# The first layer norm of the last row group, done by features instead of by rows

## The chip, the cores and the metric

The kernel runs on one core of one Trainium2 chip. The metric is the device time of one execution in microseconds (us); lower is better. All arithmetic is float32, or float32 split into a high and a low half that TensorE takes in its one-pass format (called fp32r in the rows of the profile).

## The reference

A transformer block with a modulated layer norm, 2048 rows of 448 features, 16 heads of 28:

```python
mod = (silu(c) @ w_mod).reshape(1, 6, 1, 448)
sa, ca, ga, sb, cb, gb = (mod[:, i] for i in range(6))
h = layernorm(x) * (1 + ca) + sa          # first norm
x = x + ga * attention(h, wqkv, wo)
h = layernorm(x) * (1 + cb) + sb
x = x + gb * gmlp(h, w_in, w_sp, b_sp, w_out)
```

`layernorm` is over the 448 features of a row, `(x - mean) / sqrt(var + eps)`. The change touches the first norm alone, and of it the last quarter of the rows.

## The kernel before, in words

The kernel is one program with its order written out by hand: each engine runs its instructions in the order in which the code issues them, and tiles wait for one another by semaphores. All DMAs that matter here go out on SyncE's queue (SP), also in order; each of eight semaphores of that queue is used in turn, so an issue can also wait for the DMA eight places before it.

The rows are handled in four groups g of 512. For each group the first norm makes `hT[g]`, the normalised rows turned so that features lie on the partitions: four blocks c of 128 features (the fourth has 64, held twice), each as a high half (`hi`) and a low half (what `hi` leaves out). TensorE (PE) then uses `hT[g]` for V (`v_tile`, four per group, 11 matmuls each) and for Q and K (`qk_unit`, seven per group, 11 matmuls each, of which only two per group are done ahead of the attention for g of 1 to 3). The order on PE in the stretch of interest is: V tiles 8 and 9 (g = 2), 16 transposes of group 3, V tiles 10 and 11, four matmuls that sum the modulation (`mod_sum`), Q/K units 0 and 3 of group 2, the same two of group 3, V tiles 12 to 15, another four sums, and then the first row maxima of the attention (`m_mm`, tile `mt`) woven into the other Q/K units.

How the norm of a group g is made:

- `load_x` brings 512 rows, four per partition. VectorE (DVE) takes mean and variance of each row (`ln_stat`), GpSimd (POOL) makes `rs = (var + eps) ** -0.5` (`rstd_of`, two instructions).
- `ln_norm`: DVE makes `xn = (x - mean) * rs`, four instructions, each followed by a small copy on ScalarE (ACT).
- `ln_transpose`: PE turns `xn` with 16 transposes into four PSUM banks; for each block c, ACT makes the full value with the modulation as scale and bias (`hfull`, line 118) and the high half (line 125), and DVE the low half (line 82).

`ln_next(g)` is called once for each g of 1 to 3, for 2 and 3 after two of the V tiles of group g - 1. It transposes group g and, between the blocks, takes the statistics of group g + 1. For g = 3, where no group follows, it calls `mod_split(1, ...)` after block c = 2 instead: ACT makes two high halves `acc_h`, POOL two low halves `acc_l`, and the four matmuls of `mod_sum` (line 260) read them. Their results go to `bc_ga` (DVE, line 264) and through a row in memory to `col_sb` (DVE line 268, SP lines 269 and 272).

`mod_acc(pair, k)` are DVE steps that multiply weights by `silu(c)` and add up. `pads(0, ...)` are DVE and POOL memsets (lines 574 to 576) of the first head's K and Q tiles `kst`, `qst`; the DMAs of `load_head` (lines 585 and 587) that fill these tiles wait for them, and the first `mt` matmul waits for those DMAs.

Of the kernel before, what the change touches and what calls it, by code (L numbers as in the profile page):

```python
# [8 lines left out]
F32 = mybir.dt.float32  # L9
F32R = mybir.dt.float32r  # L10
AF = mybir.ActivationFunctionType
ALU = mybir.AluOpType
# [8 lines left out]
NG = 4  # L21
# [9 lines left out]


@with_exitstack
def tile_adaln_mha_gmlp(ctx, tc, x, wqkv, wo, w_in, w_spT, b_sp, w_out, cT, w_mod0, w_mod, out):
# [6 lines left out]
    scr = ctx.enter_context(tc.tile_pool(name="scr", bufs=1, space=DRAM))  # L41
# [15 lines left out]
    cols = {}  # L57
# [23 lines left out]
    def sub(eng, dst, a, hi):  # L81
        eng.tensor_tensor(out=dst, in0=a, in1=hi.bitcast(F32), op=ALU.subtract)  # L82
# [16 lines left out]
    def rstd_of(var, rs, n):  # L99

        pool.tensor_scalar(out=rs, in0=var, scalar1=EPS, scalar2=None, op0=ALU.add)
        pool.tensor_tensor(out=rs, in0=rs, in1=mhalf[:, :n], op=ALU.pow)

    def ln_transpose(xns, full_pool, dsts, scol, bcol, engs, los=(pool,) * 4, mid=None, after=None):

        tps = []
        for c in range(4):
            tp = bank("tp")
            tps.append(tp)
            for t in range(4):  # L110
                pe.transpose(tp[:, t * 128 : (t + 1) * 128], xns[t][:, c * 128 : (c + 1) * 128], ident)  # L111
        if mid:
            mid()
        for c in (0, 2, 1, 3):
            tp = tps[c]
            f = full_pool.tile([128, 512], F32, name="hfull")
            if engs[c] is act:
                act.activation(f, tp, AF.Identity, scale=scol[:, c : c + 1], bias=bcol[:, c : c + 1])
            else:
                engs[c].tensor_scalar(  # L120
                    out=f, in0=tp, scalar1=scol[:, c : c + 1], scalar2=bcol[:, c : c + 1], op0=ALU.mult, op1=ALU.add
                )
            hi = dsts[:, c if c < 3 else 6, :]
            if engs[c] is act:
                act.activation(hi, f, AF.Copy)
# [24 lines left out]
    e1 = early.enter_context(tc.tile_pool(name="e1", bufs=2))  # L150
# [28 lines left out]
    def load_x(g, eng):  # L179
        xg = e1.tile([128, 4, D], F32, name="xg")  # L180
        for t0, t1 in ((0, 1), (1, 2), (2, 4)) if g == 0 else ((0, 4),):
            (act if t1 - t0 == 1 else eng).dma_start(xg[:, t0:t1, :], x[g, :, t0:t1])
        for t in range(4):
            xts[4 * g + t] = xg[:, t, :]

# [59 lines left out]
    def mod_split(pair, eng, pool_l, tag_l, bufs_l):  # L245

        acc = accs.pop(pair)
        accs[pair] = []
        for part in range(2):
            h = stage.tile([128, 512], F32R, name="acc_h", tag="qf")[:, :D]  # L250
            l = pool_l.tile([128, D], F32R, name="acc_l", tag=tag_l, bufs=bufs_l)
            act.activation(h, acc[:, part, :], AF.Copy)
            sub(eng, l, acc[:, part, :], h)
            accs[pair].append((h, l))

    def mod_sum(pair, part):

        pc = bank("pc")
        for i, a in enumerate(accs[pair][part]):
            pe.matmul(pc[:, :D], ones_r, a, start=i == 0, stop=i == 1)  # L260
        return pc[:, :D]

    def mod_bc(nm, pair, part):
        dve.tensor_copy(bcs[nm], mod_sum(pair, part))

    def mod_col(nm, pair, part, plus1):
        row, dst = e2.tile([1, D], F32, name="row"), scr.tile([D], F32, name=f"{nm}_scr")
        dve.tensor_scalar(out=row, in0=mod_sum(pair, part)[0:1], scalar1=plus1, scalar2=None, op0=ALU.add)
        sp.dma_start(dst.rearrange("(o n) -> o n", o=1), row)
        for r, e, c in ((0, 128, slice(0, 3)), (0, 64, slice(3, 4)), (64, 128, slice(3, 4))):  # L270
            src = dst[0:384] if e - r == 128 else dst[384:D]
            sp.dma_start(cols[nm][r:e, c], src.rearrange("(c p) -> p c", p=e - r))

    mv1, xn1 = {}, {}

    def ln_stat(g, ts):
        if g not in mv1:
            mv1[g] = e1.tile([128, 4, 2], F32, name="mv"), e1.tile([128, 4], F32, name="rs")
        for t in ts:
            st = e1.tile([128, 6], F32, name="st", bufs=4)  # L280
            dve.bn_stats(out=st, in_=xts[4 * g + t])
            dve.bn_aggr(out=mv1[g][0][:, t, :], in_=st)
# [40 lines left out]
    def v_tile(kt):  # L323
        v_copy(*v_mm(kt))
# [212 lines left out]
    def ln_step(g, t):  # L537
        ln_stat(g, (t,))
        if t % 2:
            ln_rs(g, t - 1, t + 1)  # L540

    def ln_next(g):

        if g + 1 < NG:
            ln_transpose(
                xn1.pop(g), e1, hT[g], cols["ca"], cols["sa"], (act,) * 4, (dve,) * 4, None,
                lambda c: ln_step(g + 1, (0, 2, 1, 3).index(c)),
            )
# [13 lines left out]
    for g in range(1, NG):  # L562
        if g == 3:
            early.close()
            stk = att.enter_context(tc.tile_pool(name="stk", bufs=1))
            kq = [[stk.tile([128, S], F32R, name=f"{n}st{i}") for n in "kq"] for i in range(3)]
            kst, qst = [a[0] for a in kq], [a[1] for a in kq]
            npool = att.enter_context(tc.tile_pool(name="npool", bufs=2))
            late_s = ExitStack()
            late_l = late_s.enter_context(tc.tile_pool(name="late_l", bufs=2))  # L570

            def pads(i, eng):

                dve.memset(kst[i][64:128, :].bitcast(F32), 0.0)
                eng.memset(qst[i][64:128, :].bitcast(F32), 0.0)
                pool.memset(kst[i][64:86, :].bitcast(F32), 1.0)

            pads(0, dve)

            def load_head(h, c0=0, c1=S):  # L580
                k, q = kst[h % 3], qst[h % 3]
                if h > 2:
                    sp.dma_start(q[84:86, :].bitcast(F32), q[86:88, :].bitcast(F32))
                for r0, i in ((0, 0), (56, 1), (28, 0)):
                    sp.dma_start(k[r0 : r0 + 28, c0:c1].bitcast(F32), qk_scr[i][D + h * DH : D + (h + 1) * DH, c0:c1])
                for r0, i in ((0, 0), (28, 1), (56, 0)):
                    sp.dma_start(q[r0 : r0 + 28, c0:c1].bitcast(F32), qk_scr[i][h * DH : (h + 1) * DH, c0:c1])
# [12 lines left out]
        if g + 1 < NG:  # L600
            ln_next(g + 1)
        for k in range(2):
            v_tile(4 * g + 2 + k)
            if g == 2 and k == 1:
                mod_bc("ga", 1, 0)
                mod_col("sb", 1, 1, 0.0)
            if g == 1 or g == 2 and k == 1:
                mod_acc(g, k if g == 1 else 0)
        if g < 3:
            for k, m in enumerate((0, 3)):  # L610
                qk_unit((m,), g)
                mod_acc(g, 3 - g + k)
            if g == 2:
                mod_acc(g, 3)
# [887 lines left out]
```

## Time and profile before

| what | value |
|---|---|
| three runs | 1394.78, 1395.45 and 1396.0 us, median 1395.45 |
| the profiled execution | 1395.17 us, of which 1393.4 us are the span of its instructions |
| busy: PE / PE weight load / DVE / ACT / POOL | 100% / 71% / 74% / 56% / 21% of the span |
| TensorE clock granted | full, in all 40 slices |

A row of a timeline reads: start, length, engine, line, operation, output <- input, how many, and in brackets how long the engine had been idle before it and what ended that. A row of the chain of waits reads: start, length, what. A row of a group ends with its busy time, the mean ns of one, and the idle time before. A row of windows reads: the stretch, its length, the busy time (and number) on PE, PE weight load, DVE, ACT and POOL, the granted clock, the share of the DMA engines, and GB/s. "SPq" is SyncE's DMA queue: its rows show an issue, not the transfer.

### The profile page before, as it was taken

The page shows a single profiled execution, that of the slowest core. Times are in us where ns is not written, and L with a number is a line of the kernel's source. Part 1 is how long each engine was busy: PE and PEld are TensorE (multiplying, and loading weights), DVE is VectorE, ACT ScalarE, POOL GpSimd, SP SyncE. Part 2 cuts the span into 40 slices and gives each one's busy share as a digit, 9 for nine tenths or more (in the row PEclk, how much of TensorE's full clock was granted, in tenths as well). Part 3 has the DMA queues.
Part 4 walks back from the last instruction along what each step waited for, and adds up shares of the span by engine and source line. Part 5 has one row for each costly group of instructions (what it writes and reads, how often), then busy time and mean ns, then how long its engine had stood idle before and what let it go on. Part 6 is the DMA issues. An engine that isn't in the chain of part 4 may idle for free.

```text
span 1393.4 us, 20303 instructions
## 1 busy us (share of the span) xinstructions
PE 1388.3 (100%) x7170; PEld 988.5 (71%) x7170; DVE 1024.4 (74%) x1742; ACT 779.9 (56%) x1498; POOL 286.2 (21%) x306
## 2 busy tenths in 40 slices
PE   9999999999999999999999999999999999999998
PEld 8888655555555555555555555988998888888888
DVE  7798888888888888888888851850366655668574
ACT  6623677766666777777777779363234544434211
POOL 2144212221224243323200021000142430000000
PEclk9999999999999999999999999999999999999999
DMA  8464644655465556555323002434103333445453
GB/s 285 143 177 173 188 115 151 176 169 156 152 174 162 166 163 185 165 160 155 108 68 78 20 18 72 165 119 140 46 9 105 112 111 110 143 138 164 142 171 113
DMA packets 99489, 187.01 MB, mean 134 GB/s; under 512 B 17656, under 2 KB 29434, under 8 KB 96842
## 3 DMA queue, kind: packets, MB, share of 16 engines
q1 hardware_dynamic: 96670, 181.42, 43.0%
q10 hardware_dynamic: 2718, 4.30, 0.8%
q8 instruction: 56, 0.92, 0.3%
q14 instruction: 45, 0.37, 0.1%
HBM read 130.42 MB, written 50.46 MB: 130 GB/s over the span
## 4 chain that ended last, share of the span: by engine, by line
PE 98%; DMA 1%; DVE 0%; SPq 0%; POOL 0%; issue 0%; ACT 0%
PE st_ps L671 19%; PE o_ps L686 17%; PE mt L639 17%; PE acc L1246 7%; PE acc L1247 7%; PE acc L1248 7%; PE z_ps L1172 5%; PE z_ps L1058 5%; PE pq L335 5%; PE wo_ps L927 3%; PE pv L317 2%; PE y_ps L1353 2%; PE y_ps L1352 2%; PE y_ps L1354 2%; PE tp L111 1%; DMA xg<-in_x_dram 1%
## 5 line engine op out<-in xcount | busy, mean ns | idle before, releaser
L644 DVE TENSOR_REDUCE pm<-mt 128x1 f32<-128x512 f32 x1024 | 631.0, 682 | 85.9 <-PE mt L639 85.8
L675 ACT ACTIVATE P<-st_ps 128x512 f32<-128x512 f32 x1024 | 514.6, 632 | 201.7 <-PE st_ps L671 201.7
L671 PE MATMUL st_ps<-qst,kst 128*128 128x512 f32 x1024 | 404.4, 406 | 0.0
L639 PE MATMUL mt<-kst,qst 128*128 128x512 f32 x1024 | 402.4, 393 | 0.0
L671 PEld LDWEIGHTS st_ps<-qst,kst 128*128 128x128 f32 x1024 | 191.2, 187 | 141.1 <-issue 93.1
L686 PE MATMUL o_ps<-P,V 128*32 128x512 f32 x2048 | 247.1, 598 | 0.0
L639 PEld LDWEIGHTS mt<-kst,qst 128*128 128x128 f32 x1024 | 192.4, 188 | 31.8
L790 POOL TENSOR_TENSOR ws_raw<-ws_raw 128x512 f32<-128x512 f32 x80 | 103.1, 1289 | 293.5 <-DMA ws_raw<-in_w_spT_dram 293.4
L1134 ACT ACTIVATE wsp_h<-raw_sp 128x512 fp32r<-128x512 f32 x112 | 69.9, 631 | 153.5 <-PE acc L1248 104.0
L686 PEld LDWEIGHTS o_ps<-P,V 128*32 128x32 f32 x2048 | 54.6, 109 | 122.9 <-issue 114.6
L82 DVE TENSOR_TENSOR wsp_l<-raw_sp,wsp_h 128x512 fp32r<-128x512 f32 x112 | 80.6, 729 | 82.1 <-ACT wsp_h L1134 81.4
L1246 PE MATMUL acc<-wsp_h,heapA 128*128 128x512 f32 x224 | 87.3, 390 | 0.0
L1247 PE MATMUL acc<-wsp_l,heapA 128*128 128x512 f32 x224 | 87.2, 389 | 0.0
L1248 PE MATMUL acc<-wsp_h,heapA 128*128 128x512 f32 x224 | 87.2, 389 | 0.0
L1247 PE MATMUL acc<-wsp_l,heapB 128*128 128x512 f32 x174 | 67.7, 389 | 0.0
L1248 PE MATMUL acc<-wsp_h,heapB 128*128 128x512 f32 x174 | 67.7, 389 | 0.0
L1246 PE MATMUL acc<-wsp_h,heapB 128*128 128x512 f32 x174 | 67.7, 389 | 0.0
L335 PE MATMUL pq<-heapD,heapD 128*128 128x512 f32 x196 | 61.9, 390 | 0.0
L1176 DVE BATCH_NORM_STATS2 stz<-z 128x6 f32<-128x448 f32 x32 | 19.9, 625 | 50.4 <-ACT z L1175 29.8
L1246 PEld LDWEIGHTS acc<-wsp_h,heapA 128*128 128x128 f32 x224 | 42.1, 188 | 9.0 <-DVE cD L1252 0.3
L1248 PEld LDWEIGHTS acc<-wsp_h,heapA 128*128 128x128 f32 x224 | 42.0, 188 | 8.7
L1247 PEld LDWEIGHTS acc<-wsp_l,heapA 128*128 128x128 f32 x224 | 42.1, 188 | 8.5
(225 smaller groups left out, 1597.5 us busy)
## 6 DMA issues: line engine op xcount, KB each, us to landing
ws_raw<-in_w_spT_dram SPq DMA_DIRECT2D x160, 256.0 KB
ws_scr<-ws_raw SPq DMA_DIRECT2D x80, 256.0 KB
raw_sp<-ws_scr SPq DMA_DIRECT2D x80, 256.0 KB
kst<-qk_scr SPq DMA_DIRECT2D x45, 224.0 KB
qst<-qk_scr SPq DMA_DIRECT2D x45, 224.0 KB
raw_sp<-in_w_spT_dram SPq DMA_DIRECT2D x32, 256.0 KB
qk_scr<-qh SPq DMA_DIRECT2D x28, 256.0 KB
qk_scr<-ql SPq DMA_DIRECT2D x28, 256.0 KB
```

Source lines behind the costliest of these rows:

```text
L82: eng.tensor_tensor(out=dst, in0=a, in1=hi.bitcast(F32), op=ALU.subtract)
L335: pe.matmul(pq, wqk[:, b, m * 128 : (m + 1) * 128], hT[g][:, a, :], start=j == 0, stop=j == NST - 1)
L639: pe.matmul(mt, qst[h % 3][:, t * 128 : (t + 1) * 128], kst[h % 3][:, kb * 512 : (kb + 1) * 512], start=True, stop=True)
L644: dve.tensor_reduce(out=pms[h][:, t, kb : kb + 1], in_=mt, axis=AX.X, op=ALU.max)
L671: pe.matmul(st, kst[h % 3][:, kt * 128 : (kt + 1) * 128], qst[h % 3][:, qb * 512 : (qb + 1) * 512], start=True, stop=True)
L675: act.activation(p, st, AF.Exp, scale=SCALE)
L686: pe.matmul(otile[h][32 * qb : 32 * qb + 32, :], V[:, kt, h, :], ptiles.pop((u, qb)), start=kt == 0, stop=kt == NT - 1)
L790: pool.tensor_tensor(out=a, in0=a, in1=b, op=SUMS[i // 16][2])
L1134: act.activation(hi, raw, AF.Copy)
L1246: pe.matmul(acc[i], zh, hi, start=st == 0, stop=False)
L1247: pe.matmul(acc[i], zh, lo, start=False, stop=False)
L1248: pe.matmul(acc[i], zl, hi, start=False, stop=st == 7)
```

## The change

For group 3 the norm is done with the features on the partitions from the start. The host also lays out rows 1536 to 2047 turned (`xT`, four blocks of 128 features by 512 rows, the last block's 64 features twice), and once more by rows, with four neighbouring rows on each partition (`xs`). The statistics still come from the rows. POOL makes `rs` for all 512 rows at once; DVE makes `mr = -mean * rs`; both go to a scratch row in memory (each partition writes the 16 bytes of its four rows), and come back as two tiles `rows[0]` and `rows[1]`, the same 512 numbers on all 128 partitions. `ln_rank(c)` is two DVE instructions, `xc = xc * (1 + ca) * rs` and `xc = mr * (1 + ca) + xc`; `ln_fin(c)` is one on ACT (the high half, with `sa` as bias) and one on DVE (the low half). The 16 transposes, the eight ACT instructions on their results, the four of `ln_norm` and its four copies, and the four low halves of line 82 are gone for this group. `mod_split(1, ...)` now stands behind V tile 10.

```diff
     def load_x(g, eng):
...
-            (act if t1 - t0 == 1 else eng).dma_start(xg[:, t0:t1, :], x[g, :, t0:t1])
+            (act if t1 - t0 == 1 else eng).dma_start(xg[:, t0:t1, :], x[g, :, t0:t1] if g < 3 else xs)
...
+    def load_xT():
+        for c in (0, 2, 1, 3):
+            xcs[c] = e1.tile([128, 512], F32, name="xc", tag="xn", bufs=4)
+            sp.dma_start(xcs[c], xT[c])
+
+    def ln_rows(g):
+
+        mv, rs = mv1[g]
+        rstd_of(mv[:, :, 1], rs, 4)
+        mr = e1.tile([128, 4], F32, name="mr")
+        dve.scalar_tensor_tensor(out=mr, in0=mv[:, :, 0], scalar=-1.0, in1=rs, op0=ALU.mult, op1=ALU.mult)
+        dst = scr.tile([2, 512], F32, name="ln_scr")
+        for i, v in enumerate((rs, mr)):
+            sp.dma_start(dst[i].rearrange("(p t) -> p t", t=4), v)
+        for i in range(2):
+            rows.append(e1.tile([128, 512], F32, name="lnrow", tag="hfull"))
+            sp.dma_start(rows[i], dst[i].rearrange("(o n) -> o n", o=1).broadcast_to([128, 512]))
+
+    def ln_rank(c):
+        xc, a = xcs[c], cols["ca"][:, c : c + 1]
+        dve.scalar_tensor_tensor(out=xc, in0=xc, scalar=a, in1=rows[0], op0=ALU.mult, op1=ALU.mult)
+        dve.scalar_tensor_tensor(out=xc, in0=rows[1], scalar=a, in1=xc, op0=ALU.mult, op1=ALU.add)
+
+    def ln_fin(c):
+        xc, hi, b = xcs.pop(c), hT[3][:, c if c < 3 else 6, :], cols["sa"][:, c : c + 1]
+        act.activation(hi, xc, AF.Identity, bias=b)
+        r = slice(0 if c < 3 else 64, 128)
+        o = hT[3][:, 3 + c, :] if c < 3 else hi[r]
+        dve.scalar_tensor_tensor(out=o, in0=xc[r], scalar=b[r], in1=hi.bitcast(F32)[r], op0=ALU.add, op1=ALU.subtract)
+
     def ln_next(g):
 
-        if g + 1 < NG:
-            ln_transpose(
-                xn1.pop(g), e1, hT[g], cols["ca"], cols["sa"], (act,) * 4, (dve,) * 4, None,
-                lambda c: ln_step(g + 1, (0, 2, 1, 3).index(c)),
-            )
+        ln_transpose(
+            xn1.pop(g), e1, hT[g], cols["ca"], cols["sa"], (act,) * 4, (dve,) * 4, None,
+            lambda c: ln_step(g + 1, (0, 2, 1, 3).index(c)) if g == 1 else ln_stat(g + 1, ((0, 2, 1, 3).index(c),)),
+        )
+        if g == 1:
             ln_norm(g + 1, range(4))
         else:
-            ln_transpose(
-                xn1.pop(g), e1, hT[g], cols["ca"], cols["sa"], (act,) * 4, (dve,) * 4, None, lambda c: c == 2 and mod_split(1, pool, e1, "wm", 4)
-            )
+            load_xT()
+            ln_rows(g + 1)
...
-        if g + 1 < NG:
-            ln_next(g + 1)
+        if g == 1:
+            ln_next(2)
         for k in range(2):
+            if g == 2:
+                if k == 0:
+                    ln_rank(0)
+                    ln_rank(2)
+                    ln_fin(0)
+                else:
+                    ln_rank(1)
+                    ln_fin(2)
             v_tile(4 * g + 2 + k)
+            if g == 2 and k == 0:
+                mod_split(1, pool, e1, "wm", 4)
             if g == 2 and k == 1:
+                ln_rank(3)
+                ln_fin(1)
                 mod_bc("ga", 1, 0)
                 mod_col("sb", 1, 1, 0.0)
+                ln_fin(3)
             if g == 1 or g == 2 and k == 1:
                 mod_acc(g, k if g == 1 else 0)
```

More of the change, by code (lines that the diff above doesn't have):

```diff
@@ L33, in tile_adaln_mha_gmlp @@
 @with_exitstack
-def tile_adaln_mha_gmlp(ctx, tc, x, wqkv, wo, w_in, w_spT, b_sp, w_out, cT, w_mod0, w_mod, out):
+def tile_adaln_mha_gmlp(ctx, tc, x, xs, xT, wqkv, wo, w_in, w_spT, b_sp, w_out, cT, w_mod0, w_mod, out):
     nc = tc.nc
@@ L540, in ln_step @@
             ln_rs(g, t - 1, t + 1)
-    def ln_next(g):
-        if g + 1 < NG:
-            ln_transpose(
-                xn1.pop(g), e1, hT[g], cols["ca"], cols["sa"], (act,) * 4, (dve,) * 4, None,
-                lambda c: ln_step(g + 1, (0, 2, 1, 3).index(c)),
-            )
+    xcs, rows = {}, []
+    def load_xT():
[23 more added lines that the diff above has]
+        dve.scalar_tensor_tensor(out=o, in0=xc[r], scalar=b[r], in1=hi.bitcast(F32)[r], op0=ALU.add, op1=ALU.subtract)
+    def ln_next(g):
+        ln_transpose(
[3 more added lines that the diff above has]
+        if g == 1:
             ln_norm(g + 1, range(4))
         else:
-            ln_transpose(
-                xn1.pop(g), e1, hT[g], cols["ca"], cols["sa"], (act,) * 4, (dve,) * 4, None, lambda c: c == 2 and mod_split(1, pool, e1, "wm", 4)
-            )
+            load_xT()
+            ln_rows(g + 1)
     ln_next(1)
@@ L1462 @@
     cT[:64, 3] = cT[64:, 4] = _np.asarray(inputs["c"]).reshape(448)[384:]
+    xt = _np.asarray(inputs["A_x"])[0][1536:].T
     wm = _np.asarray(inputs["w_mod"]).reshape(448, 3, 2, 448)
@@ L1479 @@
         "x": _np.asarray(inputs["A_x"])[0].reshape(4, 4, 128, 448).transpose(0, 2, 1, 3),
+        "xs": _np.asarray(inputs["A_x"])[0][1536:].reshape(128, 4, 448),
+        "xT": _np.stack([xt[:128], xt[128:256], xt[256:384], _np.concatenate([xt[384:], xt[384:]])]),
         "wqkv": twice(inputs["A_wqkv"]),
```

## The prediction

> **What bounds the kernel now.** First the page's chain of work that ended last: it is TensorE nearly all the way, so a microsecond that TensorE gains or waits goes to the end one to one. Then that chain in order of time, around the change.
>
> ```profile
> PE 98%; DMA 1%; DVE 0%; SPq 0%; POOL 0%; issue 0%; ACT 0%
> ```
>
> ```profile
> 55.71 1.75 PE tp L111 x16
> 57.46 4.49 PE pv L317 x22
> 61.95 0.81 PE pc L260 x4
> 62.76 9.99 PE pq L335 x44
> ...
> 82.75 0.23 PE mt L639
> ```
>
> From 55.71 on PE goes from stretch to stretch with nothing between, up to the first row maximum at 82.75. Now the timelines of the engines beside it: DVE, then POOL.
>
> ```profile
> 49.96 0.18 DVE L282 BATCH_NORM_AGGREGATE mv<-st 128x2 f32<-128x6 f32 x1
> ...
> 52.44 0.68 DVE L235 TENSOR_SCALAR acc<-wm,silu 128x896 f32<-128x896 f32 x1
> ...
> 56.49 1.27 DVE L243 SCALAR_TENSOR_TENSOR acc<-wm,silu,acc 128x448 f32<-128x448 f32 x2
> ...
> 71.98 1.76 DVE L574 MEMSET kst<- 64x2048 f32 x1 [0.49 <-DVE acc L243]
> ```
>
> ```profile
> 24.75 0.59 POOL L101 TENSOR_SCALAR rs<-mv 128x4 f32<-128x4 f32 x1 [0.54 <-DVE mv L282]
> 25.42 1.33 POOL L102 TENSOR_TENSOR rs<-rs,mhalf 128x4 f32<-128x4 f32 x1
> ...
> 59.51 2.34 POOL L82 TENSOR_TENSOR acc_l<-acc,acc_h 128x448 fp32r<-128x448 f32 x2 [7.95 <-ACT acc_h L252]
> ```
>
> The last statistics are ready at 50.14, DVE's modulation work between ends at 57.76, and POOL's low halves for the four sums at 61.85: the third and fourth sums of the chain (62.35 to 62.76) have them with half a microsecond to spare. That is the one thing off PE that is close to it.
>
> **Part one, what goes.** The 16 transposes are 1.75 us of the chain. If nothing else is late, PE reaches the four sums at 55.71 + 4.49 = 60.20 instead of 61.95, and all behind it moves up by 1.75. The gain can be no more than that, 0.13% of the run.
>
> **Part two, what the rows now wait for.** The queue first, and the DMA windows.
>
> ```profile
> 43.16 2.01 SPq L171 DMA_DIRECT2D wm<-in_w_mod_dram  x4
> ...
> 64.48 0.29 SPq L269 DMA_DIRECT2D sb_scr<-row  x1
> 65.63 0.41 SPq L272 DMA_DIRECT2D col_sb<-sb_scr  x1
> ...
> 76.61 1.19 SPq L587 DMA_DIRECT2D qst<-qk_scr  x3
> ...
> 574.91 0.81 SPq L786 DMA_DIRECT2D ws_raw<-in_w_spT_dram  x2
> ...
> 708.83 0.35 SPq L706 DMA_DIRECT2D r_scr<-rt  x1
> 710.97 0.59 SPq L712 DMA_DIRECT2D rb<-r_scr  x1
> ```
>
> ```profile
> 578.77 1.29 POOL L790 TENSOR_TENSOR ws_raw<-ws_raw 128x512 f32<-128x512 f32 x1 [3.03 <-DMA ws_raw<-in_w_spT_dram]
> ```
>
> ```profile
> 43.00:50.00 7.00, 7.00 (x34) 6.04 (x33) 5.62 (x13) 5.28 (x9) 1.28 (x2) 1.00 0.99 320
> 50.00:54.00 4.00, 4.00 (x21) 3.59 (x20) 3.36 (x7) 2.21 (x7) 1.24 (x2) 1.00 0.01 4
> 76.00:81.00 5.00, 5.00 (x27) 4.60 (x26) 4.14 (x6) 1.59 (x4) 1.92 (x2) 1.00 0.80 194
> ```
>
> The `xT` blocks are four DMAs of 256 KB, 1.05 MB, issued behind the modulation weights (from 45.17). These keep the DMA engines full at 320 GB/s until 50; at that rate `xT` takes 3.3 us more, to 53.3, where now they idle (4 GB/s).
>
> POOL makes `rs` for four columns at once: 0.59 + 1.33, from 50.23 to about 52.2 (the two-column pair that it replaces let DVE's `xn` end just before 52.44, so DVE's next work starts as before). `rs` is issued at 52.25, `mr` about 0.4 later. A one-row write and the next issue that waits for it are 65.63 - 64.48 = 1.15 apart, a write of 128 rows of 64 bytes and the broadcast that waits for it 710.97 - 708.83 = 2.14. No row has 128 rows of 16 bytes; their count, not their bytes, is that of the second, so I take 2.14 (`rs` landed at 54.4) and keep 1.15 as the lower end (53.4). The upper end puts the rest of `xT` ahead of it in the same queue: 53.3 + 2.14 = 55.4. Since part of `xT` is surely ahead, I take 54.75, a third of the way from 54.4 to 55.4. Then the two tiles, 256 KB each: two loads of that size issued at 574.91 let the reader of the second start at 578.77, 3.86 later. So both tiles are there at about 54.75 + 3.8 = 58.55 (57.3 to 59.3 by the two ends).
>
> DVE is free for them at 57.76, so it is a near tie, and both lead to the same point. The prices come from the groups by form, in the stretch 40 to 90:
>
> ```profile
> L82 DVE TENSOR_TENSOR ql<-pq,qh 128x512 fp32r<-128x512 f32 x8 | 5.3, 687 | 2.3 <-ACT qh L348 2.3
> L237 DVE SCALAR_TENSOR_TENSOR acc<-wm,silu,acc 128x896 f32<-128x896 f32 x4 | 4.6, 1146 | 0.0
> L125 ACT ACTIVATE heapD<-hfull 128x512 fp32r<-128x512 f32 x8 | 5.1, 633 | 0.3
> L321 ACT ACTIVATE V<-pv 128x448 f32<-128x448 f32 x12 | 6.2, 544 | 6.4 <-PE pv L317 6.4
> L243 DVE SCALAR_TENSOR_TENSOR acc<-wm,silu,acc 128x448 f32<-128x448 f32 x4 | 2.6, 680 | 0.0
> L252 ACT ACTIVATE acc_h<-acc 128x448 fp32r<-128x448 f32 x4 | 2.1, 565 | 0.0
> ```
>
> The same DVE operation is 680 ns on 448 columns and 1146 on 896, so on 512 about 0.75; an instruction that doesn't need the one before starts some 0.08 ahead of its end (the pair at 56.49: 1.27 for two of 0.68). A `ln_rank`, two of which the second needs the first, is then about 1.45, the DVE half of `ln_fin` 0.67.
>
> **Part three, the wait that replaces the transposes.** The first `ln_rank` runs from 57.8 and needs `rows[1]` at 58.6: it ends at 59.35. ACT's next instruction is the high half of `ln_fin(0)`, which waits for that. Queued behind it on ACT are the copy of V tile 10, long finished on PE, and then `mod_split`, on which PE's four sums hang: 59.35 + 0.63 (high half) + 0.5 (copy) + 0.55 (first `acc_h`) = 61.05, POOL starts 0.1 later and takes 2.34 for both low halves: 63.45, against 61.85 before. PE, there at 60.2, waits for the last of them and starts the Q/K units at about 63.75, against 62.76: **1.0 later**, not 1.75 earlier. The cover that `mod_split` had, ACT with its inputs ready, is gone.
>
> **Part four, DVE up to the attention.** From 59.35 DVE has three more `ln_rank` (4.35), four low halves (2.7), `bc_ga` and the row (at most 0.68 each by the 448-column row, 1.2 with the overlap): 67.6. hT[3] is needed by PE at 63.75 + 5.0 (two units of the 9.99) = 68.75, so that is covered by 1.1. Behind it stand `mod_acc` and two low halves of Q/K: 0.68 + 0.69 + 1.15 + 0.69 + 1.15 + 1.27 = 5.6 less overlaps of 0.3, and the 0.49 that the memset waits: the first memset starts at about 73.4, against 71.98, 1.4 later. DVE, which idled between these steps before, no longer does. The `kst`/`qst` DMAs follow the memsets, so the last issue moves from 77.8 to 79.2. How near is the first `mt`, at 82.75? The six transfers of the first head are 6 x 168 KB = 1.03 MB; from 76 to 81 the engines moved 194 x 5 = 0.97 MB. So the loads are in only just before `mt` now. With the DMAs 1.4 later and PE 1.0 later, `mt` may wait another 0 to 0.4.
>
> **The sum.** +1.0 at the four sums, +0.3 at the first `mt`: **+1.3 us**. From there PE leads again and nothing takes it back. The profiled execution would be 1395.17 + 1.3 = 1396.5; the median of the runs stands 0.28 above it, so 1396.8.
>
> **A rule that speaks against the change.** While it waits at the sums, from 60.2 to 63.5, PE has three short matmuls. No row here shows PE so idle: in each of the windows above it is busy for the whole stretch at a granted clock of 1.00. The Trainium skill, page "TensorE: Matmul & The Clock Gate", section "Part 1: The HAM clock gate", says that the array's clock falls to half after an idle window of about 3.4 us and recovers after as long a busy one. By that page the sum would hold, if these few matmuls count as activity, and be a rival (the third below) if they don't.
>
> **The rivals.**
> 1. *The wait doesn't bite, about no change (1395.0 to 1395.9).* If the rows land by 57.3 and DVE and ACT hand over a little faster than I add up, the sums start 0.5 earlier, and the slack before `mt` swallows the rest. For it: the lower ends above. Against it: DVE is free at 57.76 at best, so the sums end 0.9 later even with rows that cost nothing. A real gain of 1.75 (1393.7) also needs the memsets of the first head to move up, and these stand behind 7 us of new DVE work.
> 2. *Slower, by late rows.* DVE and ACT stand in line behind `rows[0]`, so beyond 58.6 each microsecond of landing is one of the total. Two things could do it: 256 reads of one 2 KB row from all 16 DMA engines at once, and the 16-byte writes, of which no row gives the price. One row hints at it: the broadcast of 256 KB issued at 710.97 is a DMA of the same bytes with its readers' row repeated 32 times; its use comes 5.6 later.
>
> ```profile
> 716.62 1.29 POOL L715 TENSOR_TENSOR osb<-osb,rb 128x512 f32<-128x512 f32 x1 [29.76 <-DMA rb<-r_scr]
> ```
>
>    At that price the tiles are there at 54.75 + 5.65 + some 0.5 for the second = 60.9, 2.3 late: 1396.8 + 2.3 = 1399.1. It decides, that is passes 0.2%, from a landing at about 60.1.
> 3. *Slower, by the clock.* If the wait of 3.3 us at the sums is followed by as long a stretch at half the clock, a stretch that does half the work loses half of 3.3, 1.65: 1398.4. Beside it, the page named above.
> 4. *The change does nothing on PE* would need the transposes to stay; they are gone from its list of instructions, so I give it nothing.
>
> **How the numbers follow.** The forecast, 1396.8, has 0.62; rival 1 has 0.14, rival 2 0.19, rival 3 0.05. What a measurement of this kernel can tell from no change is about 0.2%, 2.8 us: 1392.7 to 1398.2. The forecast, with a spread of 1 us, lies inside but for 0.03; rival 1 lies inside but for 0.02 on the fast side; of rival 2 about 0.04 lies inside, of rival 3 0.01. So slower 0.03 + 0.15 + 0.04 = 0.22, faster 0.02, the same 0.76. The range goes from 1395.3, which takes in half of rival 1, to 1399.2, which takes in rival 2 at its price.
>
> **What would show it.** Right: no `tp` stretch at 55.71; PE idle for about 3 us before the third or fourth `pc` of line 260, with POOL `acc_l` as what ended it; ACT waiting for DVE `xc` before its first line-569 instruction; the first memset at 73 to 74; the first `mt` about 1.3 later. Wrong: `acc_l` done by 61, PE at the Q/K units before 62.76, or DVE idle for long in front of its first line-564 instruction with a DMA of `lnrow` named (that is rival 2). A granted clock under 1.00 between 63 and 70 is rival 3.

## The result and the profile after

| | before | after |
|---|---|---|
| runs | median 1395.89 us (1394.78 to 1397.30) | median 1400.57 us (1399.50 to 1403.34) |
| ratio | | 1.0039, 95% interval 1.0028 to 1.0049 |
| profiled execution / its span | 1395.17 / 1393.4 us | 1402.46 / 1400.6 us |
| mean granted TensorE clock of the profiled run | 1.000 | 0.995 |

The change costs 4.7 us, where +1.3 was forecast. (The ratios and their intervals stand here and below as the record gives them; they are estimates from the runs and not quotients of the medians.) Times of the two traces cannot be set side by side as they stand, since the profiled execution of after was late before the change begins. These are the first matmuls of V tile 8, the last point that both have in common, before first:

```profile
51.06 4.65 PE L317 MATMUL pv<-wv,heapD 128*128 128x448 f32 x22
...
82.59 0.40 PE L639 MATMUL mt<-kst,qst 128*128 128x512 f32 x1
```

```profile
54.07 9.12 PE L317 MATMUL pv<-wv,heapD 128*128 128x448 f32 x44
64.85 0.47 PE L260 MATMUL pc<-acc_h,ones_r 128*128 128x448 f32 x1 [1.65 <-ACT acc_h L252]
66.33 0.74 PE L260 MATMUL pc<-acc_l,ones_r 128*128 128x448 f32 x1 [1.00 <-POOL acc_l L82]
66.86 0.57 PE L260 MATMUL pc<-acc_h,ones_r 128*128 128x448 f32 x1
67.88 0.74 PE L260 MATMUL pc<-acc_l,ones_r 128*128 128x448 f32 x1 [0.44 <-POOL acc_l L82]
...
90.38 0.40 PE L683 MATMUL mt<-kst,qst 128*128 128x512 f32 x1
```

After stands 3.01 us late at V tile 8. The windows of after show a granted clock of 0.50 for the whole of 12 to 16 us, before's 1.00; two experiments that differ from after only later than 40 us (e4 and e8) have such a stretch in their traces too and the others have not, so it belongs to the execution, not to the change. The measure used from here on is therefore local: **from the first matmul of V tile 8 to the first `mt`: 31.53 us before, 36.31 after, +4.78**. From `mt` to the end of the span the two differ by 0.6 (1310.8 and 1310.2). That +4.78 lies so near the 4.7 of the medians is in part chance, since the six executions of after have mean clocks from 0.995 to 0.999. To set a row of after on before's times, take 3.01 off.

The chain of waits of after, in order of time:

```profile
67.88 0.74 PE pc L260
68.62 11.91 PE pq L335 x44
80.53 8.96 PE pv L317 x44
89.50 0.81 PE pc L260 x4
90.31 0.23 PE pq L335
90.54 0.23 PE mt L683
```

The 44 Q/K matmuls start at 68.62 - 3.01 = 65.61, against 62.76 before: +2.85. And they take 11.91 instead of 9.99: +1.92. That is the whole of the 4.78. The windows (granted clock third from the end) say why they take longer:

```profile
65.00:66.00 1.00, 0.32 (x1) 0.03 (x1) 1.00 (x2) 1.00 (x3) 1.00 (x1) 0.85 0.00 0
66.00:67.00 1.00, 0.68 (x2) 0.50 (x2) 0.96 (x2) 0.31 (x1) 1.00 (x2) 0.50 0.00 0
...
71.00:72.00 1.00, 1.00 (x4) 0.81 (x3) 1.00 (x3) 0.24 (x1) 0.00 (x0) 0.50 0.00 0
72.00:73.00 1.00, 1.00 (x5) 0.82 (x4) 0.95 (x2) 0.00 (x0) 0.00 (x0) 0.74 0.07 18
```

From the shares 0.85 and 0.74 the clock is halved from 65.7 to 72.5, 6.8 us; 3.9 of these lie on the Q/K matmuls, and half of 3.9 is the 1.9 lost. It begins while PE waits at the four sums; the rest of the 6.8 is spent in that wait and on the last two sums.

The engines that PE waits for, in after: SP's queue, POOL, ACT, DVE.

```profile
54.66 0.33 SPq L557 DMA_DIRECT2D ln_scr<-rs  x1
55.08 0.38 SPq L557 DMA_DIRECT2D ln_scr<-mr  x1
57.44 0.80 SPq L560 DMA_DIRECT2D lnrow<-ln_scr  x2
```

```profile
64.88 2.95 POOL L82 TENSOR_TENSOR acc_l<-acc,acc_h 128x448 fp32r<-128x448 f32 x2 [10.24 <-ACT acc_h L252]
```

```profile
63.18 0.72 ACT L569 ACTIVATE heapD<-xc,col_sa 128x512 fp32r<-128x512 f32 x1 [3.87 <-DVE xc L565]
63.81 0.53 ACT L321 ACTIVATE V<-pv 128x448 f32<-128x448 f32 x1
64.23 1.03 ACT L252 ACTIVATE acc_h<-acc 128x448 fp32r<-128x448 f32 x2
```

```profile
61.61 0.75 DVE L564 SCALAR_TENSOR_TENSOR xc<-xc,col_ca,lnrow 128x512 f32<-128x512 f32 x1 [1.54 <-PE pv L317]
62.39 0.75 DVE L565 SCALAR_TENSOR_TENSOR xc<-lnrow,col_ca,xc 128x512 f32<-128x512 f32 x1
...
65.17 1.65 DVE L564 SCALAR_TENSOR_TENSOR xc<-xc,col_ca,lnrow 128x512 f32<-128x512 f32 x1
66.86 1.51 DVE L565 SCALAR_TENSOR_TENSOR xc<-lnrow,col_ca,xc 128x512 f32<-128x512 f32 x1
...
76.27 0.69 DVE L82 TENSOR_TENSOR ql<-pq,qh 128x512 fp32r<-128x512 f32 x1 [0.78 <-ACT qh L348]
...
79.82 1.76 DVE L605 MEMSET kst<- 64x2048 f32 x1 [0.49 <-DVE acc L243]
```

Here `heapD` is the buffer in which `hT` lies. The row norms go out at 54.66, come back into the two tiles at about 62, and the first `ln_rank` ends at 63.14. ACT, idle for 3.87, then does one high half and one V copy ahead of the two `acc_h`, and POOL's two low halves take 2.95 where they took 2.34 before. While POOL does these, the two DVE instructions beside it take 1.65 and 1.51 where their likes take 0.75. A row of before had the sign of it already: POOL's two low halves ran there from 59.51 to 61.85, DVE was idle for most of that time, and its one instruction that began beside them took 1.14, where its likes take 0.69:

```profile
61.26 1.14 DVE L82 TENSOR_TENSOR heapD<-hfull,heapD 128x512 fp32r<-128x512 f32 x1 [1.57 <-ACT heapD L125]
```

In the timeline of after `PE pv`, named as what ended DVE's wait at 61.61, had long been done; that the tiles came last is read from e2 below, where the DMA of a tile is named. So the wait at the sums is the one forecast, longer; and the memset of `kst`, last in DVE's queue, is at 79.82 - 3.01 = 76.81, against 71.98 before: **+4.83, as late as PE itself**. That second number turned out to matter as much as the first.

### The profile page after: what moved, and what is told of

It reads as the page before. It is cut to its first block, busy times and chain, and to the rows that moved or that the text cites. A ratio compares the mean times of both kernels' runs of the same rounds, so it can differ in the third digit from the quotient of the medians.

```text
span 1400.6 us, 20280 instructions
## 1 busy us (share of the span) xinstructions
PE 1391.2 (99%) x7154; PEld 989.4 (71%) x7154; DVE 1029.7 (74%) x1747; ACT 777.2 (55%) x1490; POOL 286.4 (20%) x304
## 4 chain that ended last, share of the span: by engine, by line
PE 95%; DVE 0%; issue 0%
PE st_ps L715 18%; PE o_ps L730 17%; PE mt L683 17%; PE acc L1290 6%; PE acc L1291 6%; PE acc L1292 6%; PE z_ps L1216 5%; PE z_ps L1102 5%; PE pq L335 4%; PE wo_ps L971 3%; PE y_ps L1397 2%; PE y_ps L1396 2%; PE y_ps L1398 2%; PE pv L317 1%; PE tp L111 1%; PE mtp L704 0%
```

## The experiments

All are told in one table, each number from the rows of its own trace: from V tile 8's first matmul to the first Q/K matmul behind the sums ("units"), to the memset of `kst`, to the first `mt`; how long PE idled just before that `mt`; and the median with its ratio to before, run beside it (95% interval).

| kernel | units | memset | `mt` | idle before `mt` | median us | ratio |
|---|---|---|---|---|---|---|
| before | 11.54 | 20.92 | 31.53 | 0 | 1395.89 | |
| after | 14.35 | 25.75 | 36.31 | 0 | 1400.57 | 1.0039 (1.0028 to 1.0049) |
| e1 split first | 9.78 | 23.70 | 34.13 | 3.0 | 1400.75 | 1.0037 (1.0025 to 1.0049) |
| e2 fill | 13.99 | 24.63 | 34.62 | 0.5 | 1399.94 | 1.0030 (1.0020 to 1.0041) |
| e3 rows early | 12.64 | 23.53 | 34.09 | 0 | 1398.49 | 1.0021 (1.0011 to 1.0030) |
| e4 less DVE work | 9.79 | 21.48 | 32.75 | 1.6 | 1396.74 | 1.0002 (0.9992 to 1.0011) |
| e5 low halves on DVE | 13.04 | 24.14 | 34.42 | 0.3 | 1399.27 | 1.0026 (1.0016 to 1.0035) |
| e6 sums' products ahead | 11.20 | 22.78 | 34.61 | 2.7 | 1399.63 | 1.0025 (1.0016 to 1.0035) |
| e7 and low halves on DVE | 9.78 | 22.49 | 33.08 | 2.6 | 1399.36 | 1.0019 (1.0009 to 1.0028) |
| e9 and reads on ACT | 9.78 | 21.77 | 32.11 | 1.2 | 1395.68 | 1.0002 (0.9993 to 1.0012) |
| e8 and last product late | 9.78 | 20.06 | 30.74 | 0.3 | 1395.95 | 1.0008 (0.9999 to 1.0017) |
| e10 and all reads on ACT | 9.78 | 20.08 | 30.30 | 0 | 1394.37 | 0.9997 (0.9988 to 1.0005) |
| e11 before, reads on ACT | 11.54 | 20.99 | 31.53 | 0 | 1395.53 | 1.0003 (0.9994 to 1.0012) |

Two regularities are worth seeing first. Wherever PE does not wait at the sums, the units start at 9.78 or 9.79: the 1.76 of the transposes is then really won. And the first `mt` comes 10.0 to 10.7 us behind the start of DVE's memset of `kst` in eleven of the thirteen kernels, whatever PE does: the loads of the first head wait for the memsets, DVE's and then POOL's of the same tile.

The two others, e4 with 11.3 and e6 with 11.8, show a second gate. In SP's queue the stores of group 2's Q and K (`qk_scr`) stand ahead of these loads, which read what they wrote: in all thirteen traces the first load is issued 2.8 to 3.2 us behind the last store. In e6 this comes after the memsets are done; in e4 and e7 the two come to about the same, since POOL's memset of `kst` ends 0.5 and 0.4 us behind the first load's issue. In the other ten the loads wait for POOL's memset.

**e1: the split ahead of the norm.** `mod_split(1, ...)` is moved in front of the first `ln_rank`, so that ACT and POOL can do it while the rows are under way.

```diff
             if g == 2:
                 if k == 0:
+                    mod_split(1, pool, e1, "wm", 4)
                     ln_rank(0)
...
-            if g == 2 and k == 0:
-                mod_split(1, pool, e1, "wm", 4)
```

> The modulation split (two high halves on ScalarE, two low halves on GpSimd) stands ahead of the first rank step instead of behind V tile 10. Measure: from V tile 8's first matmul to the first row maximum, 31.5 us before and 36.3 in the changed kernel. Theory A (the order on ScalarE makes TensorE wait at the four sums, and the halved clock follows from that wait): the four sums follow V tile 11 without a wait, the granted clock stays 1.00 there, and the wait moves to the first row maximum, which hangs on VectorE's longer work: 33.5 to 35, total 1398 to 1399.5. Theory B (the rows from memory hold TensorE whatever the order): it waits just as long, now at the Q/K units of group 3, total 1400 to 1401. If nothing else were late: 29.8, total 1394.

The wait at the sums and the half clock behind it are gone from the trace (units at 9.78). That is Theory A, and 34.13 lies in its range. But PE now idles 3.0 us in front of the first `mt`, and 0.9 in front of a Q/K matmul of group 3: of 4.6 us gained at the units 2.2 are left at `mt`. The median is as high as after's, above the 1398 to 1399.5 of the theory. The profiled run, with a mean clock of 1.000, took 1398.63; the other five have mean clocks of 0.995 to 0.999 and took 1400.0 to 1403.9. So the order at the sums was a cause, and a second limit stands right behind it.

**e2: PE kept busy.** After, with 18 matmuls whose result nothing reads in front of the sums.

```diff
             if g == 2 and k == 1:
                 ln_rank(3)
                 ln_fin(1)
+                fill = ps_o.tile([128, 512], F32, name="fill", tag="o")
+                for _ in range(18):
+                    pe.matmul(fill[:, :D], ones_r, wv[:, 0, :], start=True, stop=True)
```

> 18 matmuls of 448 columns whose result nobody reads (3.7 us) stand on TensorE behind V tile 11, where it waits. Theory A (idling halves the clock, and that costs about 1.9 us of the loss): the granted clock stays 1.00 from 60 to 75, the 44 matmuls of the Q/K units take 10.0 us instead of 11.9, total 1 to 2.4 us below the changed kernel, 1398.2 to 1399.6. Theory B (the halved clock is hidden, since VectorE's memsets hold the first row maximum anyway): the 44 matmuls are at full clock and the total stays within 0.5 of 1400.6. Theory C (the clock has another cause): it falls all the same, and the total is the same or 1 us more.

The chain of waits of this run:

```profile
65.23 0.47 PE pc L260
65.71 9.99 PE pq L335 x44
75.70 8.96 PE pv L317 x44
84.66 0.81 PE pc L260 x4
86.17 0.47 PE mt L686
```

With the wait filled, the sums come as late as before (units 13.99 against 14.35), but the 44 matmuls take 9.99 again: all of the half clock is gone, 1.7 of the 4.78. Adding work on PE made the kernel faster than after in the local measure. A single trace could be whole by chance, but the eight executions of e2 have mean clocks of 0.998 to 1.000, four of them 1.000, and none of after's six is over 0.999. The medians differ by 0.6 only, and their intervals overlap, so the gain is shown for the stretch and not for the total; not every execution of after need have lost the whole 1.9. The same chain, further up, has the price of the way through memory: 2.83 for the write of 16-byte rows, 4.15 for the tiles.

```profile
52.12 2.83 DMA ln_scr<-rs
...
55.00 0.32 SPq L560
...
55.45 4.15 DMA lnrow<-ln_scr
```

**e3: rows that need not wait.** The two tiles are read from the input while `xT` is loaded, so that nothing waits for the way through memory; they hold other numbers than the norm's.

```diff
     def load_xT():
         for c in (0, 2, 1, 3):
...
+        for i in range(2):
+            rows.append(e1.tile([128, 512], F32, name="lnrow", tag="hfull"))
+            sp.dma_start(rows[i], xT[i][0:1, :].broadcast_to([128, 512]))
```

> The two broadcast tiles are read from two rows of the input, right behind the four turned blocks, instead of from the scratch row, so that nothing waits for the way through memory (the tiles hold other numbers than the powers and means; the small writes stay). Theory A (the order on ScalarE is the main loss, the way through memory a small part): the first rank step starts when VectorE is free, 0.8 to 1 us earlier, the sums follow 0.8 to 1 earlier, the clock still falls; total 1399.5 to 1400. Theory B (the rows' way through memory is the main loss): 3 us or more come back, total at or below 1397.5.

Units 1.7 earlier than in after, `mt` 2.2 earlier, median 2.1 under after's; half the slowdown stays. This is between the two expectations. DVE could begin `ln_rank` at 57.36 here, as soon as its own queue was free, and ACT's and POOL's order alone still made the units 1.1 later than before. This trace too has a stretch of half clock behind the wait at the sums, of 3.4 us (from the shares 0.87 in 63:64 and 0.93 in 67:68), and its 44 matmuls take 11.40.

**e4: e1 with less work in front of the memset.** As e1; two of DVE's products of the third modulation sum are left out, so its numbers are not the reference's.

> The kernel with the split first, and two of the four multiply-add steps of the second modulation pair left out (two VectorE instructions of 1.15 us between the norm's work and the first head's memsets; that modulation is then incomplete). Measure as before: V tile 8 to the first row maximum, 34.1 us with the split first, of which TensorE waits 3.1 in front of the row maximum. Theory A (VectorE's longer work holds the memsets, the memsets the first head's transfers, these the row maximum): the memset comes 2.0 to 2.3 us earlier and the wait shrinks by as much, 31.8 to 32.1; total 1396 to 1398. Rival (the transfers are late by themselves, through the queue or the stores ahead of them): the wait stays at 2.5 to 3.1, total as with the split first.

```diff
                 qk_unit((m,), g)
-                mod_acc(g, 3 - g + k)
+                if g == 1:
+                    mod_acc(g, 3 - g + k)
+                else:
+                    wms.pop((2, 1 + k))
```

Memset 2.2 earlier than in e1, idle before `mt` 1.6 instead of 3.0, `mt` 1.4 earlier, median level with before. DVE's queue up to the memset is the second limit: less work in it, on nothing that PE reads here, takes the slowdown away. Theory A had 31.8 to 32.1 for `mt`, though. Of the 2.2 only 1.4 arrived, since the stores now hold the first load: it goes out at 24.73 behind V tile 8's first matmul, as in e1 (24.64), where POOL's memset ended only at 27.48 and here ends at 25.24.

**e5: POOL's part of the split given to DVE.** After, with one word changed.

```diff
-                mod_split(1, pool, e1, "wm", 4)
+                mod_split(1, dve, e1, "wm", 4)
```

> The changed kernel with the two low halves of the split on VectorE instead of GpSimd, at the same place in the order. Theory A (the rank steps and GpSimd's low halves, running together, slow each other: 1.65 and 1.51 us for rank steps that take 0.75 alone, 2.95 for two low halves that took 2.34): no rank step is over 0.8, the low halves take 0.62 each, the last of the four sums comes about 1 us earlier, total 0.7 to 2 below the changed kernel, 1398.6 to 1399.9. Rival (the long rank steps come from something else, such as landing transfers): the long steps stay, and VectorE's extra 1.2 us makes it 1400.6 to 1401.8.

DVE's timeline beside after's:

```profile
61.89 0.75 DVE L572 SCALAR_TENSOR_TENSOR heapD<-xc,col_sa,heapD 128x512 fp32r<-128x512 f32 x1
62.55 1.15 DVE L82 TENSOR_TENSOR acc_l<-acc,acc_h 128x448 fp32r<-128x448 f32 x2
63.62 0.75 DVE L564 SCALAR_TENSOR_TENSOR xc<-xc,col_ca,lnrow 128x512 f32<-128x512 f32 x1
64.41 0.75 DVE L565 SCALAR_TENSOR_TENSOR xc<-lnrow,col_ca,xc 128x512 f32<-128x512 f32 x1
```

DVE took on 1.15 us of work and still came to the memset 1.6 us sooner (24.14 against 25.75): with POOL silent every `ln_rank` instruction is back at 0.75, which is 1.66 for the two that were slowed. Most of the rest is the 0.78 that DVE waited for a Q/K unit in after: the stretch of half clock is shorter here (3.4 us), the units come 1.3 sooner, and DVE waits for none.

**e6: the work of the modulation ahead of the rows.** As e1, with three of the four products of the third sum moved to where DVE waits for the rows (collected in place, in the buffer of the first weights), and the last `ln_fin` ahead of the reads of the sums.

```diff
         rstd_of(mv[:, :, 1], rs, 4)
+        mod_acc(2, 0)
+        mod_acc(2, 1)
         mr = e1.tile([128, 4], F32, name="mr")
...
                     mod_split(1, pool, e1, "wm", 4)
+                    mod_acc(2, 2)
                     ln_rank(0)
```

> Split first; of the second modulation pair's steps two stand where VectorE waits for the powers and one where it waits for the rows (1.5 us each), collecting in place; the low half of the fourth block stands ahead of the two modulation results. Theory A (the loss is order alone: a wait at the sums, and VectorE's tail in front of the memsets): no wait at the sums, the memset 1 us earlier than in the kernel before, no wait at the row maximum, V tile 8 to the first row maximum 29.8 to 31.5; total 1394.2 to 1395.8. Rival (VectorE has too much work for any order): the wait at the row maximum stays over 1 us, total 1396.5 or more.

It did not work out: neither the 29.8 to 31.5 for `mt` nor the total of the theory came. POOL's low halves now fall on the first `ln_rank`:

```profile
59.03 3.56 POOL L82 TENSOR_TENSOR acc_l<-acc,acc_h 128x448 fp32r<-128x448 f32 x2 [5.53 <-ACT acc_h L254]
```

```profile
59.92 1.66 DVE L568 SCALAR_TENSOR_TENSOR xc<-xc,col_ca,lnrow 128x512 f32<-128x512 f32 x1
61.61 1.53 DVE L569 SCALAR_TENSOR_TENSOR xc<-lnrow,col_ca,xc 128x512 f32<-128x512 f32 x1
```

The sums wait for POOL again (0.9), and the memset gains 0.9 over e1, where the work moved ahead of the rows is 0.68 + 1.15 + 1.15 = 3.0. And `mt` comes 0.5 later than in e1 though the memset is earlier, because the edit that put the last `ln_fin` ahead of the reads of the sums made the row of `sb` late. It is issued 2.7 later than in e1, the stores of group 2 stand behind it, and the first load is 2.7 later as well, when POOL's memset of `kst` is already done:

```profile
76.02 0.38 SPq L356 DMA_DIRECT2D qk_scr<-ql  x1
79.12 1.41 SPq L620 DMA_DIRECT2D kst<-qk_scr  x3
```

```profile
76.50 1.81 POOL L611 MEMSET kst<- 22x2048 f32 x1 [13.91 <-PE pv L319]
```

**e7: as e6, with the low halves on DVE too,** and the third product back in its place.

```diff
-                    mod_split(1, pool, e1, "wm", 4)
-                    mod_acc(2, 2)
+                    mod_split(1, dve, e1, "wm", 4)
```

> As the last one, but VectorE fills the wait for the rows with the two low halves of the split, so that GpSimd runs nothing beside the rank steps, and the third modulation step is back at its old place. Theory A: no rank step over 0.8 us, rank steps done 0.5 to 1.5 us earlier than in the last one, memset within 0.7 of it; total 1394.2 to 1396. Rival (VectorE has too much work for any order): 1396.5 or more.

Units at 9.78 and no DVE instruction slowed, `mt` at 33.08; but the median is in the rival's range (1396.5 or more), not the theory's. The 2.6 of idle before `mt` stay, and here the clock is halved behind it, in the windows of e7:

```profile
84.00:85.00 1.00, 0.47 (x2) 0.46 (x3) 0.97 (x2) 0.00 (x0) 1.00 (x2) 1.00 0.97 328
85.00:86.00 1.00, 1.00 (x4) 0.77 (x4) 1.00 (x3) 0.00 (x0) 1.00 (x1) 0.55 0.99 236
86.00:87.00 1.00, 1.00 (x4) 0.81 (x3) 0.99 (x2) 0.00 (x0) 1.00 (x2) 0.50 0.60 195
```

From `mt` to the end is 1313.4 in this run, against 1311.2 in e1, where a like wait left the clock whole. So this execution lost behind `mt` part of what it had gained before; how many of the ten did, the traces don't tell.

**e9 and e8: what makes `mt` wait.** Two things could hold the first head's loads: the memset at the end of DVE's queue, or SP's queue, in which group 2's Q/K stores stand behind the transfers of `sb`. In e9 ACT reads the sums of `ga` and `sb` right behind V tile 11 instead of DVE after the norm, which moves both. In e8 the last product of the third sum, 1.28 us of DVE, is also moved behind the memsets (its weights in a buffer that lives on), which moves the memset and hardly the stores (e8 also puts `row` into another buffer). The first diff is of both, the second of e8.

```diff
-                mod_bc("ga", 1, 0)
-                mod_col("sb", 1, 1, 0.0)
+                act.activation(bcs["ga"], mod_sum(1, 0), AF.Copy)
+                mod_col("sb", 1, 1, 0.0)
+                ln_rank(3)
+                ln_fin(1)
+                ln_fin(3)
...
+        if nm == "sb":
+            act.activation(row, mod_sum(pair, part)[0:1], AF.Copy)
```

```diff
             pads(0, dve)
...
+            mod_acc(2, 3)
             load_head(0, 0, 1536)
```

> As e7, with the two reads of the sums (bc_ga, row) given to ScalarE right behind V tile 11, so VectorE has 1.2 us less between the rank steps and its first memset of kst, and the sb transfers leave SP's queue before group 2's stores come. Local measure: first matmul of V tile 8 to first mt, before 31.53, after 36.31, e7 33.08 with 2.6 of wait at the first mt. Theory (the memset of kst, last in VectorE's queue, decides the first head's loads): memset 1.2 earlier in the queue, 33.08 - 1.2 = 31.9 (31.6 to 32.2), wait at the first mt 1.3 to 1.6; median 1396 to 1398, lower end if the clock is not halved behind the wait as it was in e7. Rival (SP's queue decides: group 2's stores behind the sb transfers, and the loads behind the stores' landing): stores 3 us earlier, wait gone, 30.3 to 31.0; median 1394.5 to 1396.

> As e9, and the last product of the third modulation sum (1.28 us of VectorE, half rows) moved from ahead of the memsets of kst and qst to behind them, its weights in a buffer that outlives the early pool. Theory (the memset decides): memset 1.3 earlier again than in e9, wait at the first mt 0 to 0.5, measure 30.3 to 31.0, median 1394.3 to 1396.0: level with or up to 1.5 us under the kernel before (1395.9). Rival (SP's queue decides): no shorter than e9, 30.3 to 31.0 in both. If both are wrong, that is the wait stays over 1.2 us here, the loads' own time behind both gates (4.5 us for six transfers) is the limit.

The chain of waits of e9, up to `mt`, and the first loads and POOL's memset of the same run:

```profile
73.53 0.87 DVE kst L612
...
75.67 1.76 DVE qst L613
...
78.99 4.68 DMA qst<-qk_scr
...
83.87 0.47 PE mt L690
```

```profile
73.74 4.34 SPq L623 DMA_DIRECT2D kst<-qk_scr  x3
```

```profile
75.49 1.81 POOL L614 MEMSET kst<- 22x2048 f32 x1 [21.97 <-ACT V L326]
```

e9 gives 32.11, as the memset's theory said (31.9), not the 30.3 to 31.0 of SP's queue, though the transfers of `sb` went out 4.5 us sooner than in e7 and the first load 3.9 sooner: the three loads of `kst` now take 4.34 to issue, for they wait for POOL's memset. e8, with the memset 1.7 earlier, gives 30.74 with 0.3 of idle. With the stores out of the way the memset decides, and with it settled the median is level with before. The total of e8 gained less than its `mt`. The third `mt` now waited for a DVE read of the next sums behind the moved product, which is 0.5 us; from the first `mt` to the end e8's trace has 1312.6 us where before's has 1310.8, and what makes the rest of that it doesn't show.

**e10 and e11.** e8 with the last two reads of sums on ACT as well, and, to tell where a gain comes from, the kernel before with the same four reads on ACT.

```diff
-        dve.tensor_scalar(out=row, in0=mod_sum(pair, part)[0:1], scalar1=plus1, scalar2=None, op0=ALU.add)
+        act.activation(row, mod_sum(pair, part)[0:1], AF.Copy, bias=plus1)
...
-    mod_bc("gb", 2, 1)
+    act.activation(bcs["gb"], mod_sum(2, 1), AF.Copy)
```

> As e8, with the two reads of the third modulation's sums (row of cb, bc_gb) on ScalarE too, and not on VectorE behind the memsets of the other heads' buffers. In e8 the third mt stood 0.6 us later against the first than in the kernel before (1.9 against 1.4 us behind it), with the cb row's read named. Theory: that wait goes, first to third mt back to 1.4, V tile 8 to first mt 30.5 to 30.9 as in e8; sum -0.8 -0.0 against before: median 0.4 to 1.2 us under the kernel before of this call, most runs at full clock. Rival: the edit moves local times only and the total stays level with before (within 0.4), because other parts of the run take it back.

> The kernel before, no turned layout, with the same four reads of sums on ScalarE. It tells whether a gain of e10 comes from the turned layout or from these reads. The kernel before waits nowhere between V tile 8 and the first mt, so: V tile 8 to first mt 31.3 to 31.6, total within 0.3 us of before. If this kernel gains as much as e10, the turned layout gains nothing even without its waits.

e10's first `mt` is 1.23 earlier than before's, PE waits 0.2 us in the whole stretch, and its median is 0.67 under that of before, run beside it; the interval of the ratio, 0.9988 to 1.0005, contains 1. e11 has 31.53 as before has, and its median is 0.49 over before's with an interval that contains 1: the four reads alone gain nothing. So the turned layout can be made to keep most of its 1.75 where it is used, but no total that differs from before's was measured.

## Why the prediction was wrong

The forecast was 1396.8 with a range to 1399.2; the median is 1400.57. The step that failed is the wait at the four sums: its path was right, but two of its terms were too small, and the half clock behind it was left out of the sum. In the local measure, +1.3 was forecast and +4.78 came: 1.85 more at the sums, 1.92 by the clock, and 0.3 less at the first `mt`. By its steps:

- **Transposes, -1.75: right.** The `tp` stretch is gone, V tiles 8 to 11 run as one (44 matmuls, 9.12), and where nothing else waits the units start at 9.78 instead of 11.54.
- **Landing of the rows, 58.55 (57.3 to 59.3): at the upper end.** On before's times the first step starts at 58.60 and the second at 59.38, so the first `ln_rank` ends at 60.13, not 59.35, +0.8. e2's chain shows the write at 2.83, where the forecast had 2.5 (54.75 - 52.25), and a tile at 4.15, where it had 3.8 for the two.
- **ACT's order, the third part: right in kind.** ACT idled 3.87 for `xc`, then high half, V copy, `acc_h`, as listed.
- **POOL's low halves, 2.34: mis-sized.** Beside DVE's `ln_rank` they take 2.95, +0.6. With the 0.8 above, and the last sum at half clock (0.79 from the end of the last low half to the units, where the forecast had 0.3), this makes +2.85 of "+1.0 at the units". The duration was taken from a row of before beside which DVE was idle for 1.57 of the 2.34; the DVE instruction that did begin beside it, at 61.26, was itself slowed, and the prediction passed it over.
- **The clock, given 0.05 as third rival: it is 1.92 of the 4.78.** That its price, 1.65, came so near is luck: it took a stretch as long as the wait, 3.3 us, and this execution had one of 6.8, of which 3.9 lay on the Q/K matmuls. With 0.05 for it, it stood outside the sum. The prediction left it to whether three short matmuls in the wait count as activity; e2 shows that the wait is the cause, for with PE busy the clock stays whole. The Trainium skill, page "TensorE: Matmul & The Clock Gate", section "Part 1: The HAM clock gate", says that an idle window of about 3.4 us brings the half clock and a busy one ends it, and that these windows run on by themselves, not from where a wait begins. The lengths seen, 3.4 and 6.8 us, agree with one and two such windows. But PE was not idle for 3.4 us in after: the pieces are 1.65, 1.00 and 0.44 with matmuls between. Nor was it in e7, where one piece of 2.64 was followed by the half clock, and one of 2.97 in e1 was not. So less than a whole idle window was enough here, and what decides whether such a wait halves the clock no run shows.
- **DVE's queue up to the memset, 73.4: mis-sized, 76.8.** The sum of its instructions was right: in e1 it is 14.0 from the end of the first `ln_rank` to the memset, as forecast (73.4 - 59.35 = 14.05). Missing were the 0.8 above, 1.66 for the two instructions slowed by POOL, and 0.78 of waiting for the late Q/K units.
- **The first `mt`, "0 to 0.4": right by accident in after, wrong as a reading.** PE was as late as the memset, so no wait shows. e1 has the wait at 3.0. The prediction's own words, that the loads are in only just before `mt` now, were the second limit: the distance from memset to `mt` is 10.6 in before and 10.0 in e2, where PE waited for the loads, so there is some 0.6 of slack in it, and what is put in front of the memset beyond that delays `mt`.
- **Rival 2, late rows**, is not the main cause: the landing itself was at the end of the range given, not at the rival's 60.9. But rows that need not wait (e3) give 2.1 us of the median back, nearly half of the loss, by way of the wait that the rows set off.

What is shown, in the local measure: the half clock (by e2, all of it), the order at the sums (e1), POOL beside DVE (e5), the memset (e9, e8; e4 up to the point where the stores hold). That the stores in SP's queue hold the loads in e4 and e6 is read from their traces; no run moves the stores alone. What is only argued: that e1's median, level with after's, is due to the clock in executions without a trace; their mean clocks fit it.

## What to carry to other kernels

When a transfer or a layout takes work off the bounding engine, follow each engine's queue to the next point at which the bounding engine reads, and look for all of these points: here two of them, the sums and the first head's loads, had next to no slack, so most of the work put in front of them came back as waiting, and behind each gate stood another. Put work that hangs on a long round trip behind everything that is ready, not ahead of it. And price a short wait of TensorE with the clock that may follow it: a wait of 3 us cost 2 us more, at times, and in the local measure filling it with useless matmuls was cheaper than leaving it.

## What the runs showed of the hardware

- Half clock behind short waits of TensorE: for 6.8 us in after, whose wait had 3.1 us of idling in three pieces, and for 3.4 us in e3 (1.9 in two pieces), e5 (2.2 in two) and e7 (2.6 in one). It did not come in each run: e1 idled 3.0 us in one piece, e6 2.7, and both kept their clock.
- DVE's instructions that read two tiles and POOL's `TENSOR_TENSOR`, which reads two as well, slow one another: `SCALAR_TENSOR_TENSOR` on 128x512 takes 0.75 us alone and 1.51 to 1.68 beside POOL's, and POOL's two take 2.34 in before and 2.95 to 3.56 so (after, e2, e3, e6). In e1 only one DVE instruction began beside the second of POOL's; it took 1.60, and POOL's two 2.30. The Trainium skill, page "SBUF — State Buffer", section "Who interferes with whom", says that such a pair contends for one shared read port, and calls the shared ports an exclusive lock. The trace agrees with the slowing (0.75 to 1.65); that the second waits for the whole of the first it does not show.
- 512 numbers written as 16 bytes from each of 128 partitions: 2.83 us from issue to use (e2). One row of 2 KB spread over 128 partitions: 4.15 (e2).
